# Scores as three half-word products from the sixth pair on, and another placing of the MoE units between the attention steps

## The chip, the cores and the metric

The kernel runs on one NeuronCore of a Trainium2 chip. The metric is the device time of one launch in microseconds (us). The engines are PE (TensorE: matrix products and transposes), DVE (VectorE), ACT (ScalarE), POOL (GpSimd) and SP (SyncE, which issues the DMAs). Each of them works through its own queue in the order in which the program put the instructions there, and they wait for each other by semaphores.

## The reference

```python
# q, k, v: (4, 8, 576, 64); x after attention: (4, 576, 512)
q_rot, k_rot = (rotate(q), rotate(k))
scores = scale * np.matmul(q_rot, k_rot.transpose(0, 1, 3, 2))
scores = scores - np.max(scores, axis=-1, keepdims=True)
attn = np.exp(scores)
attn = attn / (np.sum(attn, axis=-1, keepdims=True) + 1e-09)
attn_out = np.matmul(attn, v)
x = attn_out.transpose(0, 2, 1, 3).reshape(B, S, H * D)
h = np.maximum(x @ w_in, 0.0)              # w_in: 512 x 1024
conv_out = sum(conv_w[k] * shifted(h, k) for k in range(3))
gate = 1.0 / (1.0 + np.exp(-conv_out))
return h * gate @ w_out                    # w_out: 1024 x 512
```

## The kernel before

**Pairs and steps.** The 32 heads are taken as 16 pairs p. Each pair has five steps s: four blocks of 128 rows of q and, in step s = 4, the last 64 rows of both heads. A global step is n = 5p + s, 80 in all. In a step PE makes the scores of both heads (`emit_S`, L251, tiles `sp` from `qT` and `kT`), DVE takes the row maximum (L259, `negm`), and ACT the exponential (L263, `st`, or `str` for s = 4). PE turns the exponentials of the step before (`emit_T`, L311, tiles `tp`), and ACT copies them to `pt` (L189). What is left over of 64 key columns is turned apart (`emit_Trem`, L336), and DVE copies that to `pt` (L191). One head uses partitions 0 to 63 of `qT` and `kT`, the other 64 to 127, so a product of one head uses half of PE's rows.

**The product with v.** `emit_E` (L367) multiplies `pt` by v for the pair p in step 5(p+1), in two halves of 290 columns. A step with n divisible by five is called an E step below. ACT copies the results to `xn` (L377), DVE normalises them two or more steps later (L381), ACT and POOL split them in a high and a low part (L385, L386, tile `xT`).

**The wide stage and the switch.** Steps below `WIDE` = 26 use large PSUM tiles and run beside the conversion of the weights (`wsteps`, 64-bit to 32-bit, then high and low parts `winh`, `winl`, `wouth`, `woutl`, on ACT, DVE and POOL). At step 26 the PSUM is dealt out anew: two tiles `s` for scores, two `t` for transposes and E, two `m` for the MoE.

**The MoE.** From step 26 on, MoE units stand between the steps' other work. A block is 288 tokens. `emit_M1` (L400, an M1 unit) makes 128 of the 1024 hidden columns for a block in 12 products: (high weight, high x), (high weight, low x), (low weight, high x) for four slices of 128. The parts have the type float32r, where PE makes one pass. A plain float32 product is two passes and shows as two records. Each M1 unit is followed on other engines by a ReLU (ACT), three convolution steps (DVE), tanh (ACT), gate (DVE) and a split (ACT, POOL, tile `g`), each put off by so many ticks (`defer`). `emit_M2` (L478, an M2 unit) makes a quarter of an output tile, six products of 512 columns.

**Order.** `plan` holds (rank, function) for each step and `moe` the units of each step. The loop sorts by rank: scores 0, turning 1, exponentials 1.5, the rest 2; MoE units are set around the events of rank 2 and 4; E of the MoE stage has rank 10 and closes its step. The units of a block are spread over ten steps by a fraction x and a `room` of each step. Transposes of q and k (L224 to L233) are DVE's, at rank 0.45. The rotation (`rope`, L180, L183) is POOL's, at the end of a step. After step 86 comes the tail, blocks 6 and 7 of the MoE, with no attention beside it.

Of the kernel before, what the change touches and what calls it, by code (L numbers as in the profile page):

```python
# [20 lines left out]
def attention_moe_kernel(ctx, tc, q, k, v, w_in, conv_w, w_out, tab, tabx, out):  # L21
# [37 lines left out]
    rvc = [keep.tile([128, 32], F32, name=f"rvc_{s}") for s in range(2)]  # L59
    cw = keep.tile([128, 32], F32, name="cw")  # L60
    vrem = keep.tile([128, 2, D], F32, name="vr")
    strem = [keep.tile([128, S + 64], F32, name=f"str_{s}") for s in range(2)]
# [122 lines left out]
    QT, KT = {}, {}  # L185

# [8 lines left out]
    def qk_tiles(p):  # L195
        if p not in QT:
            QT[p] = p2.tile([128, S], F32, tag="qT", name="qT")
            KT[p] = p2.tile([128, S + 64], F32, tag="kT", name="kT")
# [21 lines left out]
    def emit_TQ(p, part):  # L220
        qk_tiles(p)
        x = raw.pop((p, part))[:, :, 0, :]
        if part == "q":
            nc.vector.transpose(out=QT[p].rearrange("p (c i) -> p c i", i=32), in_=x)  # L224
        else:
            kt = KT[p].rearrange("p (c i) -> p c i", i=32)
            nc.vector.transpose(out=kt[:, 2:20], in_=x)  # L227
            if p * STEPS < WIDE:
# [3 lines left out]
            if p * STEPS + STEPS > WIDE:  # L232
                nc.vector.transpose(out=kt[:, 0:2], in_=x[:, 16:18])  # L233
# [10 lines left out]
    def emit_S(p, s):  # L244
# [22 lines left out]
        if s < 4:  # L267
            st = ST[p, s] = p1.tile([128, 2, S], F32, tag="st", name="st", bufs=3)
        else:
            st = STR[p] = strem[p % 2][:, 0:S]  # L270
# [33 lines left out]
    def emit_T(p, s, h=None):  # L304
# [8 lines left out]
        if s == 4:  # L313
            st = strem[p % 2]
# [46 lines left out]
    def emit_E(p, j, a=0, n=XW):  # L361
        b, hp = divmod(p, NPB)
        xp = spare(n)
# [10 lines left out]
        if a == 0:  # L374
            xns[p, j] = p2.tile([128, XW], F32, tag="xn", name="xn", bufs=4)
# [218 lines left out]
    WIDE = 26  # L594
# [8 lines left out]
    def emit():  # L603
        with tc.manual_schedule(engines=engines):
            load0()
            for x in rvc + krem + [x[:, S:S + 64] for x in strem]:
# [23 lines left out]
            for p in range(NP):  # L630
# [10 lines left out]
                if n + 4 < WIDE:  # L641
                    for i in range(4):
                        at(n + 1 + i, 2, lambda p=p, i=i: emit_Trem(p, i, 1))
                else:
                    for i in range(2):
                        at(n + 2 + 2 * i, 2, lambda p=p, i=i: emit_Trem(p, 2 * i, 2))
# [8 lines left out]
                for j in range(2):  # L655
                    at(n + (9 if j and n + 8 < WIDE else 8), 1.7 + j, lambda p=p, j=j: norms.pop((p, j))())
# [7 lines left out]
            for blk in range(2 * B - 2):  # L664
                n0 = WIDE + MB * blk
                room = [0.5 if n % STEPS == 0 and n < STEPS * NP + 2 else 1.0 for n in range(n0, n0 + MB)]
                us = [(0.09 + 0.1 * f, lambda blk=blk, f=f: emit_M1(blk, f)) for f in range(NF)]
                if blk:
                    m2 = m2_units(blk - 1)
                    ne = 4 if blk % 4 == 0 else 0  # L670
                    us += [(0.05 * i if i < ne else 0.05 * ne + (1 - 0.05 * ne) * (i - ne) / (len(m2) - ne), u) for i, u in enumerate(m2)]
                for x, u in us:
                    y, k = x * sum(room), 0
# [115 lines left out]
```

## Time and profile before

| what | value |
|---|---|
| median of 3 runs | 516.81 us (515.56 to 519.25) |
| the profiled execution's own time | 514.66 us |
| its span, first to last instruction | 512.7 us |
| PE busy | 469.0 us, 91% of the span, 3880 products |
| DVE, ACT, POOL busy | 365.0, 311.8, 300.3 us |
| mean granted TensorE clock | 0.983 of full speed |

The span is what the rows of the trace add up to. The execution's own time is 1.96 us more, for what lies around it. The median of the timed runs is 2.15 us above the profiled execution. Busy time counts an instruction from start to end, and matrix products overlap, so lengths of work on PE are read as differences of start times.

### The profile page before, as it was taken

What the parts mean: (1) busy time and instruction counts of PE and PEld (TensorE: products, weight loads), DVE (VectorE), ACT (ScalarE), POOL (GpSimd) and SP (SyncE); (2) the same over time, 40 slices, a digit from 0 to 9 for tenths busy, and PEclk for the clock granted to TensorE, in tenths of its full rate; (3) what the DMA queues carried; (4) which work ended last, traced back from release to release, by engine and by line L of the source; (5) the groups of instructions that cost most, each with busy time, mean ns of one, the idle gap of its engine ahead of it and who ended that gap; (6) DMA issues with size and microseconds to landing.
All of it is one profiled execution on the core that took longest, in us unless ns stands there. A gap on an engine that the chain in (4) does not pass through costs nothing.

```text
span 512.7 us, 10801 instructions
## 1 busy us (share of the span) xinstructions
PE 469.0 (91%) x3880; PEld 350.0 (68%) x3880; DVE 365.0 (71%) x656; ACT 311.8 (61%) x821; POOL 300.3 (59%) x479
## 2 busy tenths in 40 slices
PE   1878789786999899999999999999999999999997
PEld 1445446553766587767878687868777676889986
DVE  5699889995597759684868487765868284748951
ACT  2588877885576767675667575754657564325520
POOL 3789988999576747646492829274573021314530
PEclk9999987997999999999999999999999999999999
DMA  8978965843424243433425251524220201000011
GB/s 225 178 128 165 191 158 140 188 113 76 88 47 94 47 93 68 93 69 73 90 49 90 63 100 45 88 73 88 51 68 1 68 1 46 22 21 22 1 42 60
DMA packets 139256, 42.61 MB, mean 83 GB/s; under 512 B 132012, under 2 KB 132804, under 8 KB 139204
## 3 DMA queue, kind: packets, MB, share of 16 engines
q1 hardware_dynamic: 137860, 41.54, 37.1%
q8 instruction: 30, 0.49, 0.4%
q10 hardware_dynamic: 1344, 0.39, 0.3%
q14 instruction: 22, 0.18, 0.1%
HBM read 37.12 MB, written 4.79 MB: 82 GB/s over the span
## 4 chain that ended last, share of the span: by engine, by line
PE 67%; DVE 13%; ACT 7%; POOL 5%; DMA 5%; issue 2%; SPq 0%; ACTq 0%; DVEq 0%; POOLq 0%
PE pm L400 13%; PE sp L251 12%; PE pm L478 11%; PE tp L367 11%; PE mt L478 8%; PE mt L400 5%; PE tp L311 5%; DVE negm L259 4%; ACT st L263 3%; ACT pt L189 2%; DMA rq<-q 2%; POOL rk L180 1%; DVE c L414 1%; POOL woutl L559 1%; DMA rk<-k 1%
## 5 line engine op out<-in xcount | busy, mean ns | idle before, releaser
L259 DVE TENSOR_REDUCE negm<-sp 128x1 f32<-128x576 f32 x144 | 102.4, 747 | 73.9 <-PE sp L251 66.6
L432 POOL TENSOR_TENSOR g<-c,g 128x288 fp32r<-128x288 f32 (+4 forms) x88 | 56.8, 658 | 154.6 <-ACT g L431 151.7
L189 ACT ACTIVATE pt<-tp 128x512 f32<-128x512 f32 (+3 forms) x176 | 84.4, 528 | 53.7 <-PE tp L311 53.3
L251 PE MATMUL sp<-kT,qT 64*128 64x288 f32 (+4 forms) x556 | 104.3, 474 | 6.4 <-DVE kT L227 3.2
L263 ACT ACTIVATE st<-sp,negm 128x576 f32<-128x576 f32 x128 | 94.0, 746 | 14.6 <-DVE negm L259 14.1
L400 PE MATMUL pm<-xT,winh 128*128 128x290 f32 x384 | 81.7, 305 | 0.0
L414 DVE SCALAR_TENSOR_TENSOR c<-rr,cw,c 128x288 f32<-128x288 f32 x128 | 77.6, 606 | 4.5
L251 PEld LDWEIGHTS sp<-kT,qT 64*128 64x128 f32 (+1 forms) x556 | 47.2, 179 | 33.5 <-issue 15.4
L478 PE MATMUL pm<-wouth,g 128*128 128x512 f32 x176 | 65.8, 415 | 0.0
L400 PEld LDWEIGHTS pm<-xT,winh 128*128 128x128 f32 x384 | 62.3, 189 | 3.2 <-issue 0.4
L311 PEld LDWEIGHTS tp<-idf,st 64*128 64x128 f32 x1024 | 42.5, 140 | 27.1 <-ACT st L263 16.2
L180 POOL TENSOR_TENSOR rq<-rq,tabt 128x192 f32<-128x192 f32 x90 | 56.8, 666 | 5.5 <-DMA rq<-q 5.3
L311 PE MATMUL tp<-idf,st 64*128 64x64 f32 x1024 | 49.4, 229 | 10.5 <-ACT st L263 10.4
L400 PE MATMUL pm<-xT,winl 128*128 128x290 f32 x192 | 56.7, 296 | 0.0
L367 PE MATMUL tp<-pt,vm 128*64 128x290 f32 x384 | 53.6, 422 | 3.4 <-ACT pt L189 3.4
L180 POOL TENSOR_TENSOR rk<-rk,tabt 128x192 f32<-128x192 f32 x90 | 56.6, 665 | 0.0
L423 DVE SCALAR_TENSOR_TENSOR c<-c,rr 128x288 f32<-128x288 f32 x64 | 36.6, 575 | 15.3 <-ACT c L420 15.3
L412 DVE TENSOR_SCALAR c<-rr,cw 128x288 f32<-128x288 f32 x64 | 33.3, 521 | 18.0 <-ACT rr L408 14.0
L386 POOL TENSOR_TENSOR xT<-xn,xT 128x290 fp32r<-128x290 f32 x32 | 29.6, 940 | 24.1 <-ACT xT L385 24.1
L367 PEld LDWEIGHTS tp<-pt,vm 128*64 128x64 f32 x384 | 27.0, 140 | 23.0 <-ACT pt L189 4.4
L420 ACT ACTIVATE c<-c 128x288 f32<-128x288 f32 x64 | 28.5, 445 | 17.7 <-DVE c L414 17.5
L478 PEld LDWEIGHTS pm<-wouth,g 128*128 128x128 f32 x176 | 33.0, 188 | 8.1
(102 smaller groups left out, 797.8 us busy)
## 6 DMA issues: line engine op xcount, KB each, us to landing
out<-ot SPq DMA_DIRECT2D x17, 256.0 KB
rq<-q SPq DMA_DIRECT2D x30, 144.0 KB
rq<-q SPq DMA_DIRECT2D x60, 72.0 KB
rk<-k SPq DMA_DIRECT2D x30, 144.0 KB
rk<-k SPq DMA_DIRECT2D x60, 72.0 KB
w<-moe_w_in SPq DMA_DIRECT2D x8, 512.0 KB
vm<-v SPq DMA_DIRECT2D x32, 128.0 KB
w<-moe_w_out SPq DMA_DIRECT2D x8, 512.0 KB
```

What stands on the lines that cost most here:

```text
L180: nc.gpsimd.tensor_tensor(out=y, in0=y, in1=tabt[:, a:a + 3], op=ALU.mult)
L189: nc.scalar.activation(out=out, in_=in_, func=AF.Copy, scale=1.0 if sc is None else sc)
L251: nc.tensor.matmul(out=out, lhsT=qt[64 * h:64 * h + 64, c], rhs=kt[64 * h:64 * h + 64, a:a + n], start=True, stop=True)
L259: reds.setdefault((p, s), []).append(lambda: nc.vector.tensor_reduce(out=nm, in_=sc, axis=AX.XY if len(sc.shape) == 3 else AX.X, op=ALU.ma ...
L263: lambda: nc.scalar.activation(out=dst, in_=sc, func=AF.Exp, bias=nm, scale=1.0, accum_out=sm)
L311: nc.tensor.transpose(ps[r][:, 64 * k:64 * k + 64], x[i], idf[i, i])
L367: nc.tensor.matmul(out=xp[64 * h:64 * h + 64, :], lhsT=vmain[p][:, h, i, :] if i < 4 else vrem[:, h, :], rhs=pt[:, 2 * i + h if i < 4 else ...
L400: nc.tensor.matmul(out=ps[:, 0:XW], lhsT=w[:, kk, fs], rhs=xT[:, xs, e, :], start=(i == 0), stop=(i == n - 1))
L414: nc.vector.scalar_tensor_tensor(out=c, in0=r[:, j + e:j + e + HS], scalar=cw[:, 8 * e + f:8 * e + f + 1], in1=c, op0=ALU.mult, op1=ALU.add,)
L423: nc.vector.scalar_tensor_tensor(out=c, in0=c, scalar=1.0, in1=r[:, j + 1:j + 1 + HS], op0=ALU.add, op1=ALU.mult)
L432: nc.gpsimd.tensor_tensor(out=lo, in0=c[:, o:o + n], in1=hi.bitcast(F32), op=ALU.subtract)
L478: nc.tensor.matmul(out=ops[tt][:, 0:width], lhsT=g_tile(tt, f, e), rhs=w[:, f, cols], start=(f == 0 and i == 0), stop=(f == NF - 1 and i = ...
```

## The change

From pair 5 on (all pairs whose last step lies at or beyond `WIDE`, which is now 25) the turned q and k go to one buffer each (`turnedq`, `turnedk`). ACT copies these, rounded, to a high part (`hq`, `hk`), and DVE subtracts that to get a low part (`lq`, `lk`). The scores are three float32r products, high by high, high by low and low by high, added up in PSUM. For s = 4 the two heads' 64 rows of q stand as a block diagonal in 128 rows, and the three products use all of PE's rows.

The MoE stage begins at step 25. The first block has 8 steps, the others ten; E steps have no room for units, so the 16 or 20 units of a block go to eight steps, evenly. Both halves of E stand in one E step, and the first uses an `m` tile in place of a `t` tile. `emit_Trem` turns one block in each of four steps, where the MoE stage had two in each of two. The normalisation of a pair moves from its step n+8 to n+7. Some buffers become fewer: `st` 3 to 2, `str` 2 to 1, `xn` 4 to 2.

```diff
+    def high_low(p, part, src):
+        hi, lo = (p2.tile(list(src.shape), F32R, tag=t + part, name=t + part) for t in "hl")
+        HI[p, part], LO[p, part] = hi, lo
+        defer(2, lambda: nc.scalar.activation(out=hi, in_=src, func=AF.Copy))
+        defer(4, lambda: nc.vector.tensor_tensor(out=lo, in0=src, in1=hi.bitcast(F32), op=ALU.subtract))
...
+        split = p * STEPS + STEPS > WIDE
...
+        def mms(items, c):
+            if (p, "q") not in HI:
+                for out, h, a, n in items:
+                    mm(out, h, a, n, c)
+                return
+            (qh, kh), (ql, kl) = ((t[p, "q"], t[p, "k"]) for t in (HI, LO))
+            for i, (x, y) in enumerate(((qh, kh), (qh, kl), (ql, kh))):
+                for out, h, a, n in items:
+                    r = slice(64 * h, 64 * h + 64)
+                    nc.tensor.matmul(out=out, lhsT=x[r, c], rhs=y[r, a:a + n], start=i == 0, stop=i == 2)
...
-                for h in range(2):
-                    mm(pss_[h][:, j, 0:HS], h, HS * j + 64 - 64 * h, HS, c)
+                mms([(pss_[h][:, j, 0:HS], h, HS * j + 64 - 64 * h, HS) for h in range(2)], c)
...
-            for h, j in ((0, 0), (1, 1), (0, 1), (1, 0)):
-                mm(ps[64 * h:64 * h + 64, j, 0:HS], h, HS * j + 64, HS, c)
+            for j in range(2):
+                for i, (x, y) in enumerate(((qh, kh), (qh, kl), (ql, kh))):
+                    nc.tensor.matmul(
+                        out=ps[:, j, 0:HS], lhsT=x[:, 512:640], rhs=y[:, HS * j + 64:HS * j + 64 + HS],
+                        start=i == 0, stop=i == 2,
+                    )
...
-        xp = spare(n)
+        xp = m_tile()[:, 0:n] if "m" in psum and j == 0 else spare(n)
...
-    WIDE = 26
+    WIDE = 25
...
-                n0 = WIDE + MB * blk
-                room = [0.5 if n % STEPS == 0 and n < STEPS * NP + 2 else 1.0 for n in range(n0, n0 + MB)]
+                n0 = WIDE + MB * blk - (MB - NF if blk else 0)
+                room = [float(n % STEPS != 0 or n > STEPS * NP) for n in range(n0, n0 + (MB if blk else NF))]
```

The scores of one ordinary step and what follows them on PE, before:

```order
L251 MATMUL sp<-kT,qT 128x288 x4
L311 MATMUL tp<-idf,st 128x64 x16
L478 MATMUL pm<-wouth,g 128x512
L478 MATMUL pm<-woutl,g 128x512
L478 MATMUL pm<-wouth,g 128x512 x2
L478 MATMUL pm<-woutl,g 128x512
L478 MATMUL pm<-wouth,g 128x512
```

And now, in a step of the same kind, the scores, the turning and the begin of the M1 unit that follows:

```order
L285 MATMUL sp<-hk,hq 128x288 x2
L285 MATMUL sp<-lk,hq 128x288 x2
L285 MATMUL sp<-hk,lq 128x288 x2
L285 MATMUL sp<-hk,hq 128x288 x2
L285 MATMUL sp<-lk,hq 128x288 x2
L285 MATMUL sp<-hk,lq 128x288 x2
L347 MATMUL tp<-idf,st 128x64 x16
L436 MATMUL pm<-xT,winh 128x290 x2
```

Four products of two passes have become twelve of one pass.

An E step without MoE units on PE, before (the end of the step ahead of it stands in the first two rows):

```order
L478 MATMUL pm<-wouth,g 128x512
L336 MATMUL tp<-idf,st 128x128 x2
L251 MATMUL sp<-kT,qT 128x288 x4
L311 MATMUL tp<-idf,str_82 128x64 x10
L367 MATMUL tp<-pt,vm 64x290 x8
L367 MATMUL tp<-pt,vr 64x290 x2
L367 MATMUL tp<-pt,vm 64x290 x8
L367 MATMUL tp<-pt,vr 64x290 x2
```

And every E step now:

```order
L372 MATMUL tp<-idf,st 128x128
L514 MATMUL pm<-wouth,g 128x512
L514 MATMUL pm<-woutl,g 128x512
L514 MATMUL pm<-wouth,g 128x512 x2
L514 MATMUL pm<-woutl,g 128x512
L514 MATMUL pm<-wouth,g 128x512
...
L347 MATMUL tp<-idf,str 128x64 x10
L403 MATMUL pm<-pt,vm 64x290 x8
L403 MATMUL pm<-pt,vr 64x290 x2
L403 MATMUL tp<-pt,vm 64x290 x8
L403 MATMUL tp<-pt,vr 64x290 x2
```

A unit now stands between the leftover transpose (L336, now L372) and the next step's scores, and the first half of E writes `pm` in place of `tp`.

DVE in a step in which k is turned, before:

```order
L259 TENSOR_REDUCE negm<-sp 128x1 x2
L227 STREAM_TRANSPOSE kT<-rk 128x576
L233 STREAM_TRANSPOSE kT<-rk 128x64
L412 TENSOR_SCALAR c<-rr_1703,cw 128x288
L414 SCALAR_TENSOR_TENSOR c<-rr_1703,cw,c 128x288 x2
L381 TENSOR_TENSOR xn<-xn,rb 128x290 x2
L259 TENSOR_REDUCE negm<-sp 128x1
```

And now:

```order
L291 TENSOR_REDUCE negm<-sp 128x1 x2
L246 STREAM_TRANSPOSE turnedk<-rk 128x576
L248 STREAM_TRANSPOSE turnedk<-rk 128x64
L199 COPY pt<-tp 128x128
L459 SCALAR_TENSOR_TENSOR c<-c,rr_1650 128x288
L193 TENSOR_TENSOR lk<-turnedk,hk 128x640
L448 TENSOR_SCALAR c<-rr_1647,cw 128x288
L450 SCALAR_TENSOR_TENSOR c<-rr_1647,cw,c 128x288 x2
L291 TENSOR_REDUCE negm<-sp 128x1
```

The subtraction for `lk` and a copy of a leftover transpose have come in between two maxima; the normalisation (`xn`) has gone to another step.

## Rows read from the trace of the kernel before

**Rows 1.** Stretch, length, busy PE, weight loads, DVE, ACT, POOL, then clock, DMA.

```profile
117.74:168.54 50.80, 46.43 (x385) 32.80 (x386) 35.31 (x65) 33.33 (x87) 35.18 (x65) 0.93 0.37 74
168.54:443.94 275.40, 268.32 (x2242) 204.78 (x2243) 188.88 (x350) 171.99 (x450) 142.76 (x223) 1.00 0.29 64
```

**Rows 2.** PE in order of time, steps 37 to 39: start, length, records.

```profile
184.69 1.24 PE L251 MATMUL sp<-kT,qT 64*128 64x288 f32 x8
185.77 0.66 PE L311 MATMUL tp<-idf,st 64*128 64x64 f32 x16
...
189.78 1.24 PE L251 MATMUL sp<-kT,qT 64*128 64x288 f32 x8
191.44 0.50 PE L478 MATMUL pm<-wouth,g 128*128 128x512 f32 x1
...
192.94 0.43 PE L400 MATMUL pm<-xT,winh 128*128 128x290 f32 x2
...
194.65 1.19 PE L251 MATMUL sp<-kT,qT 64*64 64x288 f32 x8
195.77 0.71 PE L311 MATMUL tp<-idf,st 64*128 64x64 f32 x16
```

**Rows 3.** PE in order of time, a short stretch inside the first scores of Rows 2.

```profile
185.04 0.65 PE L251 MATMUL sp<-kT,qT 64*128 64x288 f32 x4
```

**Rows 4.** PE in order of time, a float32 product of all rows in the wide stage.

```profile
118.80 0.49 PE L277 MATMUL sp<-kr,qT 128*128 128x128 f32 x2
119.12 0.27 PE L336 MATMUL sp<-idf,st 128*128 128x128 f32 x1
```

**Rows 5.** PE in order of time, E step 40, with an M1 unit.

```profile
199.83 1.24 PE L251 MATMUL sp<-kT,qT 64*128 64x288 f32 x8
...
201.30 0.54 PE L400 MATMUL pm<-xT,winh 128*128 128x290 f32 x2
...
203.11 2.17 PE L367 MATMUL tp<-pt,vm 128*64 128x290 f32 x16
...
208.14 1.24 PE L251 MATMUL sp<-kT,qT 64*128 64x288 f32 x8
```

**Rows 6.** All engines in order of time, E step 45, without a unit; idle before in brackets.

```profile
226.54 1.39 PE L251 MATMUL sp<-kT,qT 64*128 64x288 f32 x8
...
228.45 0.53 PE L311 MATMUL tp<-idf,str 64*128 64x64 f32 x9 [0.52 <-DVE pt L191]
...
229.45 2.17 PE L367 MATMUL tp<-pt,vm 128*64 128x290 f32 x16 [0.47 <-ACT pt L189]
...
234.48 1.24 PE L251 MATMUL sp<-kT,qT 64*128 64x288 f32 x8
```

**Rows 7.** PE in order of time, step 31, with one M1 unit.

```profile
155.34 1.24 PE L251 MATMUL sp<-kT,qT 64*128 64x288 f32 x8
...
159.62 1.72 PE L251 MATMUL sp<-kT,qT 64*128 64x288 f32 x7 [0.73 <-ACT st L263]
```

**Rows 8.** All engines in order of time, scores of steps 25, 26 and 27.

```profile
117.74 1.13 PE L251 MATMUL sp<-kT,qT 64*128 64x512 f32 x4 [1.62 <-DVE kT L227]
...
120.17 0.74 ACT L263 ACTIVATE str<-sp,negm 128x576 f32<-128x576 f32 x1
...
127.41 1.41 PE L251 MATMUL sp<-kT,qT 64*128 64x288 f32 x8
...
133.65 1.24 PE L251 MATMUL sp<-kT,qT 64*128 64x288 f32 x8
```

**Rows 9.** Busy time, columns as in Rows 1, around step 25.

```profile
121.00:128.00 7.00, 6.42 (x34) 3.32 (x36) 2.74 (x6) 4.02 (x14) 7.00 (x14) 0.51 0.27 47
```

**Rows 10.** Groups of instructions, each shape apart: busy, mean ns.

```profile
L381 DVE TENSOR_TENSOR xn<-xn,rb 128x290 f32<-128x290 f32 x32 | 15.1, 502 | 2.8 <-ACT xn L377 2.6
...
L556 ACT ACTIVATE winh<-wf 128x512 fp32r<-128x512 f32 x8 | 5.0, 630 | 2.3 <-DVE wf L513 2.2
```

**Rows 11.** DVE in order of time, maxima of step 43.

```profile
219.37 1.42 DVE L259 TENSOR_REDUCE negm<-sp 128x1 f32<-128x576 f32 x2 [1.24 <-PE sp L251]
```

More of the change, by code (lines that the diff above doesn't have):

```diff
@@ L59, in attention_moe_kernel @@
     rvc = [keep.tile([128, 32], F32, name=f"rvc_{s}") for s in range(2)]
+    turned = {part: keep.tile([128, S + 64], F32, name=f"turned{part}") for part in "qk"}
     cw = keep.tile([128, 32], F32, name="cw")
     vrem = keep.tile([128, 2, D], F32, name="vr")
-    strem = [keep.tile([128, S + 64], F32, name=f"str_{s}") for s in range(2)]
+    strem = [keep.tile([128, S + 64], F32, name="str")]
     xT = keep.tile([128, NSLOT, 2, XW], F32R, name="xT")
@@ L196, in qk_tiles @@
         if p not in QT:
-            QT[p] = p2.tile([128, S], F32, tag="qT", name="qT")
-            KT[p] = p2.tile([128, S + 64], F32, tag="kT", name="kT")
+            QT[p] = wkeep.tile([128, S], F32, tag="qT", name="qT", bufs=2)
+            KT[p] = wkeep.tile([128, S + 64], F32, tag="kT", name="kT", bufs=2)
     def emit_TQ0(part):
@@ L220, in emit_TQ @@
     def emit_TQ(p, part):
-        qk_tiles(p)
         x = raw.pop((p, part))[:, :, 0, :]
-        if part == "q":
-            nc.vector.transpose(out=QT[p].rearrange("p (c i) -> p c i", i=32), in_=x)
-        else:
-            kt = KT[p].rearrange("p (c i) -> p c i", i=32)
-            nc.vector.transpose(out=kt[:, 2:20], in_=x)
-            if p * STEPS < WIDE:
+        split = p * STEPS + STEPS > WIDE
+        if split:
+            dst = turned[part]
+        else:
+            qk_tiles(p)
+            dst = (QT if part == "q" else KT)[p]
+        to = dst.rearrange("p (c i) -> p c i", i=32)
+        if part == "q":
+            if split:
+                nc.vector.transpose(out=to[:, 0:16], in_=x[:, 0:16])
+                for h in range(2):
+                    r = slice(64 * h, 64 * h + 64)
+                    nc.vector.transpose(out=to[r, 16 + 2 * h:18 + 2 * h], in_=x[r, 16:18])
+            else:
+                nc.vector.transpose(out=to, in_=x)
+        else:
+            nc.vector.transpose(out=to[:, 2:20], in_=x)
+            if split:
+                nc.vector.transpose(out=to[:, 0:2], in_=x[:, 16:18])
+            else:
                 for h in range(2):
@@ L231, in emit_TQ @@
                     nc.vector.transpose(out=krem[p % 2][r, r].rearrange("p (c i) -> p c i", i=32), in_=x[r, 16:18])
-            if p * STEPS + STEPS > WIDE:
-                nc.vector.transpose(out=kt[:, 0:2], in_=x[:, 16:18])
+        if split:
+            high_low(p, part, dst)
     ST, STR = {}, {}
@@ L247, in emit_S @@
             sums[p] = p2.tile([128, 9], F32, tag="sums", name="sums")
-        qt, kt = QT[p], KT[p]
+        qt, kt = QT.get(p), KT.get(p)
         def mm(out, h, a, n, c):
@@ L267, in emit_S @@
         if s < 4:
-            st = ST[p, s] = p1.tile([128, 2, S], F32, tag="st", name="st", bufs=3)
+            st = ST[p, s] = p1.tile([128, 2, S], F32, tag="st", name="st", bufs=2)
         else:
-            st = STR[p] = strem[p % 2][:, 0:S]
+            st = STR[p] = strem[0][:, 0:S]
         if "m" not in psum:
@@ L374, in emit_E @@
         if a == 0:
-            xns[p, j] = p2.tile([128, XW], F32, tag="xn", name="xn", bufs=4)
+            xns[p, j] = p2.tile([128, XW], F32, tag="xn", name="xn", bufs=2)
         xn = xns[p, j]
@@ L605, in emit @@
             load0()
-            for x in rvc + krem + [x[:, S:S + 64] for x in strem]:
+            for x in [turned["q"]] + rvc + krem + [x[:, S:S + 64] for x in strem]:
                 nc.vector.memset(x, 0.0)
@@ L640, in emit @@
                         at(m + 1, 0 if m + 1 < WIDE else 1, lambda p=p, s=s, h=h: emit_T(p, s, h))
[L641 to L646, printed above, removed]
+                for i in range(4):
+                    at(n + 1 + i, 2, lambda p=p, i=i: emit_Trem(p, i, 1))
                 if n + 8 < WIDE:
@@ L655, in emit @@
                 for j in range(2):
[L656 removed]
+                    at(n + (9 if j else 8) if n + 8 < WIDE else n + 8 - (n + 5 >= WIDE), 1.7 + j, lambda p=p, j=j: norms.pop((p, j))())
             nw = len(wsteps)
@@ L670, in emit @@
                     ne = 4 if blk % 4 == 0 else 0
-                    us += [(0.05 * i if i < ne else 0.05 * ne + (1 - 0.05 * ne) * (i - ne) / (len(m2) - ne), u) for i, u in enumerate(m2)]
-                for x, u in us:
-                    y, k = x * sum(room), 0
+                    us += [(0.05 * i if i < ne else 0.05 * ne + (1 - 0.05 * ne) * (i - ne + 0.5) / (len(m2) - ne), u) for i, u in enumerate(m2)]
+                us.sort(key=lambda e: e[0])
+                for i, (x, u) in enumerate(us):
+                    y, k = (i + 0.5) / len(us) * sum(room), 0
                     while y >= room[k]:
```

9 lines of the change are left out of this document (6 added, 3 removed).

## The prediction

> **What bounds the kernel now.** I read the stretches first, then PE in order of time. In the stretch from step 34 to the tail, 275.40 us long, PE is busy for 268.32 us, DVE for 188.88 and ACT for 171.99 [rows 1]. So PE is the bound there, and what counts is what each piece costs on PE from start to start. An ordinary step with one M1 and one M2 unit, step 38, goes from 189.78 to 194.65, 4.87 us, and nothing is idle in it. Step 37, with two leftover transposes besides, takes 189.78 - 184.69 = 5.09, so such a transpose costs 0.11. Scores take 185.77 - 184.69 = 1.08 (s = 4: 195.77 - 194.65 = 1.12), an M2 unit 192.94 - 191.44 = 1.50, an M1 unit 194.65 - 192.94 = 1.71, of which about 1.60 are its 12 products, 0.134 each, and 0.11 the wait before the next scores [rows 2].
>
> PE isn't the bound in two places. One is an E step without a unit. Step 40, with an M1 unit, takes 208.14 - 199.83 = 8.31; less its M1 unit, 203.11 - 201.30 = 1.81, that is 6.50 [rows 5]. Step 45 has no unit and takes 234.48 - 226.54 = 7.94: the transposes wait 0.52 for DVE, which empties the leftover transpose, E waits 0.47 for ACT, which empties the transposes, and the scores are slow too [rows 6]. There are five such steps (35, 45, 55, 65, 75), 1.1 to 1.6 over 6.50, 7.0 us in all. The other is a step with one unit, as 31: 159.62 - 155.34 = 4.28 for some 3.4 us of work, and its successor waits for the exponentials [rows 7]. Six steps before 34 are of this kind, each about 1 us over its work. The switch itself is a third place: from the scores of step 25 to those of 27 it is 133.65 - 117.74 = 15.9 us [rows 8], at a granted clock of 0.51 for 7 us of it, the 1.2 GHz level, after PE had been waiting for `kT` [rows 8, 9].
>
> **Scores.** A float32 step has 8 records. Four of them begin by 185.04 in two pairs, and from 185.04 on three pairs take 185.77 - 185.04 = 0.73, 0.243 a pair; the first pair takes 0.35, 0.11 more, for the load of its weights after a product of another shape [rows 2, 3]. The two heads of a pair run side by side: a float32 record of all rows costs (119.12 - 118.80)/2 = 0.16 for 128 columns [rows 4], where one of these costs 0.12 for 288. The new step has 12 records, six pairs of one pass. No row shows a float32r product on half of the rows. From below, a pair costs half of a two-pass pair, 0.122; from above, 0.134 for each head apart, 0.27 a pair, if they don't run together. I take 0.134 a pair, what one float32r product of 290 columns costs, since float32 pairs do run together. A step then costs 6 x 0.134 + 0.11 = 0.91 in place of 1.08: 0.17 less, in 43 steps from 26 on, 7.3 us (with 0.122: 10). For s = 4 six full-row products cost 0.80 in place of 1.12: 0.32 in 11 steps, 3.5 us. Sum: -10.8.
>
> The Trainium skill speaks against this, in the page "TensorE: Matmul & The Clock Gate", section "Part 3: Packing small matmuls — row/col tiling": a weight load overlaps a running matmul only where the row group differs. The new pairs come one after the other on the same two row groups, so each pair's loads would lie open by it. The trace of before doesn't agree for float32, whose pairs on the same groups follow at 0.243 with no room for a load [rows 3]; the result by that rule is the second rival.
>
> **E steps.** All 11 E steps beside scores are now without a unit. What made the five wait is treated twice: a unit of 1.5 us now stands between the leftover transpose and the next scores, so DVE's copy has 2.4 us in place of 1.1; and the first half of E takes an `m` tile, so it needn't wait until ACT has emptied the transposes, whose copies only the second half needs, 2.5 us later. I take 6 of the 7.0 us as gone. If only the first cure works, E still waits about half a us in 11 steps and the gain is 2. Norms one step earlier have E's 5 us and the next steps before them; I cost them at nothing.
>
> **Steps with one unit.** The first block now has 8 units in six steps, two of them with two: four light steps (26, 28, 29, 32) in place of six. -2 us, -1 to -3.
>
> **The switch.** Step 25's scores now need the new PSUM, so they come after the exponentials of step 24 (which begin at 120.17 and take 0.74 [rows 8]) and after two more copies on ACT and DVE for k's parts: about 122 in place of 117.74. Then both halves of E follow in that step, 6.6 us at full clock, partly at half of it as E was before [rows 9]. I get the scores of step 26 at 131.6 and of 27, with one M1 unit done, at 136, where before they stood at 133.65 with the same work done. +2.4, from -1 (a warm clock) to +5. The zeroing of `rr` on POOL moves ahead of 5 us of rotation, which takes away a wait of the first convolution, off this path.
>
> **Added work elsewhere.** For each pair ACT makes two copies of 640 columns. One of 512 takes 0.63 [rows 10], so 0.63 to 0.79 each, 1.5 a pair. DVE makes two subtractions of 640, from 0.50 (that of 290 [rows 10]) to 1.11 (in proportion), say 0.85, and splits a transpose and two copies in smaller ones: 2.4 us a pair, 1.3 to 3.4. Four units a pair in each of them, where before it was five and three, make the load even. DVE's 188.88 in 275.40 is 69% [rows 1]; nine and a half pairs at 2.4 add 23, and the stretch gets shorter, so some 83%. ACT goes from 62% to 73%. What covers this is that DVE sits at the maxima and waits for scores, as 1.24 us in step 43 [rows 11]. But the subtraction for k stands there between two maxima, and waits for its copy on ACT; behind it are the convolution, the next maximum, then the exponentials, for which the scores after that wait. The leftover transpose also takes a `t` tile in four steps of five, not two, and the next step's transposes wait for DVE's copy of it. I put +4 on this, about 0.1 a step; from 0 to +10, which is 0.2 in each of 49 steps.
>
> **Rest.** Smaller buffers (`st`, `str`, `xn`) are read a step before they are written again; the tail is unchanged, but its first M2 units come nearer to the last M1 unit, within a us. Both at nothing.
>
> **Sum.** -10.8 - 6 - 2 + 2.4 + 4 = -12.4 on the profiled 514.66: 502.3. The median of the runs lies 2.15 above that execution, so I forecast 504.4, say 504.
>
> **Rivals.** First, DVE becomes what PE waits for. For it: 83% on an engine whose instructions wait in order; against it: an M1 unit in each of steps 37 to 39 and no idle PE there [rows 2]. The added stalls are then 10 to 12 instead of 4: 511. Second, the pairs' weight loads lie open, slower than before: each pair costs 0.134 + 0.11 = 0.24, six of them 1.45, 0.37 more than the 1.08 of now. 43 steps cost 16 more where I take off 7.3; s = 4 keeps its gain, as full-row M1 products at 0.134 hide their loads. 504 + 23 = 527. It decides against the change from about 0.22 a pair on, where the other gains are used up. Were the heads not to run together, it would be 539. For it: no row shows such products; against it: the float32 pairs [rows 3]. Third, E steps wait as before, all 11 at 1.4: 15.4 in place of the 1 left above, 518. For it: six of them lose the unit that covered them [rows 5]; against it: the new tile. Last, all goes well, 0.122 a pair and no stalls: 493.
>
> **Chances.** Forecast 0.60, DVE 0.19, open loads 0.06, E steps 0.07, all well 0.08. About 1% is what a measurement of this kernel can tell from no change, 511.6 on the fast side. Nearly all of the forecast, all of the best case and most of DVE's lie below it: faster 0.77; the rest of DVE's and most of the E case within 1%: 0.15; slower 0.08. The range leaves out the open loads, the E case and half of the best: 496 to 513.
>
> **What would show it.** In the trace after: 12 score records a step with 0.9 us from the first to the turning; E steps of 6.3 to 6.6; ordinary steps of 4.7 to 4.85; the scores of step 27 near 136. Wrong if score pairs stand 0.2 or more apart, if PE's idle time names DVE's copies or subtractions in most steps, or if the switch loses more than 5 us.

## The result, and the profile after

The changed kernel takes 522.24 us (521.07 to 523.47, six runs) and the kernel before, on the same chip, 515.55 (515.22 to 519.25): a ratio of 1.0115, with a 95% interval of 1.0084 to 1.0146. It is slower by 1.15%, where 504 us was predicted. The profiled span is 520.7 us, against 512.7.

I cut each trace at the starts of the scores of steps 25, 36 and 79. The columns are the times between these cuts, in us; the experiments that stand below are in the table too.

| kernel | to step 25 | 25 to 36 | 36 to 79 | from 79 on | span | median |
|---|---|---|---|---|---|---|
| before | 117.7 | 62.1 | 238.9 | 94.0 | 512.7 | 515.6 |
| after | 126.0 | 69.9 | 238.4 | 86.4 | 520.7 | 522.2 |
| no wait (`early_no_wait`) | 124.4 | 67.9 | 229.0 | 86.4 | 507.7 | 508.9 |
| late (`lo_late`) | 122.3 | 63.0 | 226.7 | 86.4 | 498.4 | 501.3 |
| no subtraction (`no_sub`) | 122.3 | 62.6 | 226.8 | 86.3 | 497.9 | 499.6 |

What was won is in the last column: the MoE's blocks begin earlier, so that fewer units are left for the steps behind 79 (the tail itself, blocks 6 and 7, is 68.8 and 68.9 us). What was lost stands in the first two, and the long third one, in which the scores and the E steps were to give most, gave 0.5 us. Not all of the first column is the kernels' own: step 22 begins at 105.81 in the change and at 103.28 in the late version, so 2.5 of the 3.7 us between these two arise where they have the same instructions. From 82 to 90 us the granted clock is 0.71 in the change and 1.00 in the late version.

The stretches of the change, columns as in [rows 1], show it from the side of PE:

```profile
126.02:195.92 69.90, 62.78 (x538) 49.48 (x538) 51.85 (x96) 43.31 (x109) 44.53 (x76) 0.87 0.28 55
195.92:434.30 238.38, 230.11 (x2120) 185.65 (x2119) 187.08 (x357) 163.57 (x419) 130.06 (x197) 1.00 0.32 69
```

In the second PE is idle for 8.3 us (238.38 - 230.11; before it was 3.5 in the same steps, 238.89 - 235.42), and DVE is busy for 78% of it (187.08/238.38). In the first the granted clock is 0.87 of full speed.

The scores themselves are as forecast. PE in order of time, step 36 of the change (L285 are the scores, L347 the turning), answers to [rows 2, 3]:

```profile
195.92 0.40 PE L285 MATMUL sp<-hk,hq 64*128 64x288 f32 x2
196.16 0.30 PE L285 MATMUL sp<-lk,hq 64*128 64x288 f32 x2
196.29 0.29 PE L285 MATMUL sp<-hk,lq 64*128 64x288 f32 x2
196.43 0.29 PE L285 MATMUL sp<-hk,hq 64*128 64x288 f32 x2
...
196.82 0.66 PE L347 MATMUL tp<-idf,st 64*128 64x64 f32 x16
...
200.72 0.40 PE L285 MATMUL sp<-hk,hq 64*128 64x288 f32 x2
```

The second pair begins 0.24 after the first and the others 0.13 to 0.14 apart; the scores take 0.90 and the whole step 4.80. But only two steps of these five, 36 and 37, are so short. All engines in order of time, steps 37 to 40 of the change (L192 is the copy of the high part, L193 the subtraction, L448 and L450 the convolution, L291 the maximum, L295 the exponential, L332 the scores for s = 4; in brackets the idle time before and its releaser):

```profile
200.53 0.76 ACT L192 ACTIVATE hq<-turnedq 128x640 fp32r<-128x640 f32 x1
...
201.32 0.83 DVE L193 TENSOR_TENSOR lq<-turnedq,hq 128x640 fp32r<-128x640 f32 x1 [1.57 <-ACT hq L192]
...
202.47 1.07 DVE L450 SCALAR_TENSOR_TENSOR c<-rr,cw,c 128x288 f32<-128x288 f32 x2
...
203.46 1.41 DVE L291 TENSOR_REDUCE negm<-sp 128x1 f32<-128x576 f32 x2
...
206.69 0.76 PE L347 MATMUL tp<-idf,st 64*128 64x64 f32 x16
...
207.58 1.93 DVE L450 SCALAR_TENSOR_TENSOR c<-rr,cw,c 128x288 f32<-128x288 f32 x2
...
209.44 1.41 DVE L291 TENSOR_REDUCE negm<-sp 128x1 f32<-128x576 f32 x2
...
211.16 0.40 PE L332 MATMUL sp<-hk,hq 128*128 128x288 f32 x1 [0.40 <-ACT st L295]
...
211.92 0.29 PE L332 MATMUL sp<-hk,lq 128*128 128x288 f32 x1
...
212.79 0.82 DVE L193 TENSOR_TENSOR lk<-turnedk,hk 128x640 fp32r<-128x640 f32 x1 [0.59 <-ACT hk L192]
213.53 0.92 DVE L448 TENSOR_SCALAR c<-rr,cw 128x288 f32<-128x288 f32 x1
214.48 1.50 DVE L450 SCALAR_TENSOR_TENSOR c<-rr,cw,c 128x288 f32<-128x288 f32 x2
215.91 0.74 DVE L291 TENSOR_REDUCE negm<-sp 128x1 f32<-128x576 f32 x1
...
216.69 0.74 ACT L295 ACTIVATE str<-sp,negm 128x576 f32<-128x576 f32 x1 [0.17 <-DVE negm L291]
...
217.57 0.40 PE L285 MATMUL sp<-hk,hq 64*128 64x288 f32 x1 [1.08 <-ACT str L295]
```

Read it from the bottom. PE waits 1.08 us in the E step because the exponentials of step 39 are late. They are late because their maximum starts at 215.91, although the last of those scores began at 211.92. In between DVE stood still for 0.59 for ACT's copy of k, subtracted, and did three pieces of the convolution, all of which stand in its queue ahead of the maximum. One step earlier the maxima of step 38 start at 209.44, though the last of that step's scores were under way when the turning (L347) began at 206.69; that is 3.94 after the first score of 205.50. The change's order makes only a part of this: in the kernel with late subtractions below it is 3.24 (198.15 - 194.91), for there too the convolution ahead of these maxima takes 1.93. In step 37 DVE stood still for 1.57 us in the change, because `lq` waits for a copy that on ACT stands behind two exponentials and a ReLU. When it was free, most of that step's scores were done, and the subtraction and the convolution still came first: the maxima begin 2.74 after the scores (203.46 - 200.72). Before, DVE at its maxima waited for the scores, as in [rows 11]; now the scores, by way of the exponentials, wait for DVE. The waits of the stretch from 196 to 430 in the change's trace, as us in all, how often, longest:

```profile
PE sp L285 <- ACT str L295: 5.0, 6, 1.1
PE sp L332 <- ACT st L295: 1.7, 4, 0.6
DVE lq L193 <- ACT hq L192: 11.4, 8, 1.7
DVE lk L193 <- ACT hk L192: 3.4, 7, 0.6
```

The E steps, which [rows 5, 6] show at 7.94 and 8.31, are from step 40 to 75 at 7.2 to 7.8 in six of eight and at 6.34 in two. The switch, to be set against [rows 8]: scores of step 25 at 126.02 (forecast 122), of 26 at 134.64 (131.6), of 27 at 138.09 (136).

### The profile page after: what moved, and what is told of

Same layout as the page of the kernel before. It is cut to its first block, busy times and chain, and to the rows that moved or that the text cites. A ratio compares the mean times of both kernels' runs of the same rounds, so it can differ in the third digit from the quotient of the medians.

```text
span 520.7 us, 11167 instructions
## 1 busy us (share of the span) xinstructions
PE 468.5 (90%) x4036; PEld 363.9 (70%) x4036; DVE 392.5 (75%) x720; ACT 325.2 (62%) x843; POOL 304.9 (59%) x479
## 3 DMA queue, kind: packets, MB, share of 16 engines
HBM read 37.12 MB, written 4.79 MB: 80 GB/s over the span
## 4 chain that ended last, share of the span: by engine, by line
PE 49%; DVE 28%; ACT 14%; issue 5%; DMA 2%; POOL 1%; SPq 0%; DVEq 0%; ACTq 0%; POOLq 0%
DVE negm L291 8%; PE pm L403 7%; PE mt L514 6%; PE pm L436 6%; PE sp L285 6%; ACT st L295 6%; PE tp L403 6%; PE mt L436 5%; DVE c L450 5%; PE pm L514 5%; PE tp L347 4%; DVE c L448 3%; PE sp L272 2%; ACT pt L197 2%; DVE wt L544 2%
## 5 line engine op out<-in xcount | busy, mean ns | idle before, releaser
L291 DVE TENSOR_REDUCE negm<-sp 128x1 f32<-128x576 f32 x144 | 102.3, 746 | 35.8 <-PE sp L285 26.5
L468 POOL TENSOR_TENSOR g<-c,g 128x288 fp32r<-128x288 f32 (+4 forms) x88 | 58.7, 678 | 101.0 <-ACT g L467 95.8
L295 ACT ACTIVATE st<-sp,negm 128x576 f32<-128x576 f32 x128 | 93.8, 742 | 27.5 <-DVE negm L291 27.4
L450 DVE SCALAR_TENSOR_TENSOR c<-rr,cw,c 128x288 f32<-128x288 f32 x128 | 83.3, 651 | 4.5
L436 PE MATMUL pm<-xT,winh 128*128 128x290 f32 x384 | 85.7, 316 | 0.3 <-ACT rr L444 0.3
L422 POOL TENSOR_TENSOR xT<-xn,xT 128x290 fp32r<-128x290 f32 x32 | 28.4, 889 | 77.8 <-ACT xT L421 71.1
L181 POOL TENSOR_TENSOR rq<-rq,tabt 128x192 f32<-128x192 f32 x90 | 59.6, 695 | 5.5 <-DMA rq<-q 5.5
L347 PE MATMUL tp<-idf,st 64*128 64x64 f32 x1024 | 49.0, 231 | 13.1 <-ACT st L295 12.2
L347 PEld LDWEIGHTS tp<-idf,st 64*128 64x128 f32 x1024 | 42.6, 143 | 21.6 <-ACT st L295 17.0
L285 PE MATMUL sp<-hk,hq 64*128 64x288 f32 x176 | 39.4, 352 | 10.8 <-ACT str L295 6.7
L448 DVE TENSOR_SCALAR c<-rr,cw 128x288 f32<-128x288 f32 x64 | 33.6, 525 | 16.1 <-ACT rr L444 16.1
L285 PEld LDWEIGHTS sp<-hk,hq 64*128 64x128 f32 x176 | 22.0, 189 | 29.7 <-issue 8.5
L436 PEld LDWEIGHTS pm<-xT,winl 128*128 128x128 f32 x192 | 37.5, 196 | 0.0
L272 PE MATMUL sp<-kT,qT 64*128 64x512 f32 (+2 forms) x120 | 34.3, 667 | 2.2 <-DVE kT L246 1.5
```

Of the source, the lines that this page charges most:

```text
L181: nc.gpsimd.tensor_tensor(out=y, in0=y, in1=tabt[:, a:a + 3], op=ALU.mult)
L285: nc.tensor.matmul(out=out, lhsT=x[r, c], rhs=y[r, a:a + n], start=i == 0, stop=i == 2)
L291: reds.setdefault((p, s), []).append(lambda: nc.vector.tensor_reduce(out=nm, in_=sc, axis=AX.XY if len(sc.shape) == 3 else AX.X, op=ALU.ma ...
L295: lambda: nc.scalar.activation(out=dst, in_=sc, func=AF.Exp, bias=nm, scale=1.0, accum_out=sm)
L347: nc.tensor.transpose(ps[r][:, 64 * k:64 * k + 64], x[i], idf[i, i])
L436: nc.tensor.matmul(out=ps[:, 0:XW], lhsT=w[:, kk, fs], rhs=xT[:, xs, e, :], start=(i == 0), stop=(i == n - 1))
```

## The experiments

My theory after the two traces was the order: on DVE the subtraction waits for ACT's copy and holds up the next maxima, which stand behind it. The rivals were the load (DVE's added work in all, wherever it stands) and the placing (no units in E steps, two or three elsewhere). If nothing else is said, all but the edit is as in the change. The kernel before took 516.65 to 517.36 us beside these runs, and the ratios are against that.

**Where the subtraction stands (`lo_late`).** It goes behind the maxima of the next step.

```diff
-        defer(4, lambda: nc.vector.tensor_tensor(out=lo, in0=src, in1=hi.bitcast(F32), op=ALU.subtract))
+        at(late["n"] + 1, 0.25, lambda: nc.vector.tensor_tensor(out=lo, in0=src, in1=hi.bitcast(F32), op=ALU.subtract))
```

> The subtractions stay on DVE, but each is put behind the maxima of the next step instead of ahead of them. Theory 1 (order): as if they were off DVE, 500 to 508 us, steps as for the kernel with POOL. Theory 2 (load): DVE's work is the same, 516 to 522. Theory 3 (placing): within 3 us of 522.

Measured: 501.29 us, a ratio of 0.9695 (0.9644 to 0.9747), the lowest time here of a kernel that does the whole work. One moved line gives back 21 us. DVE in order of time, step 37 of this kernel and the maxima of step 38:

```profile
190.10 0.37 DVE L448 TENSOR_SCALAR c<-rr,cw 128x288 f32<-128x288 f32 x1 [0.95 <-ACT rr L444]
190.51 1.07 DVE L450 SCALAR_TENSOR_TENSOR c<-rr,cw,c 128x288 f32<-128x288 f32 x2
191.50 1.42 DVE L291 TENSOR_REDUCE negm<-sp 128x1 f32<-128x576 f32 x2
192.83 0.81 DVE L193 TENSOR_TENSOR lq<-turnedq,hq 128x640 fp32r<-128x640 f32 x1
...
198.15 1.41 DVE L291 TENSOR_REDUCE negm<-sp 128x1 f32<-128x576 f32 x2
```

The scores of the step begin at 190.11 and the maxima 1.39 later; in the change it was 203.46 - 200.72 = 2.74. The subtraction waits for nothing. All E steps from 40 on are at 6.3, and the stretches show PE idle for only 1.6 us in 226.70, although DVE has the same work and is busy for a larger share, 185.52/226.70 = 82%:

```profile
122.31:185.32 63.01, 58.29 (x539) 46.10 (x540) 51.06 (x96) 43.17 (x109) 42.90 (x72) 0.94 0.31 61
185.32:412.02 226.70, 225.07 (x2119) 183.76 (x2118) 185.52 (x358) 162.17 (x419) 132.54 (x203) 1.00 0.33 73
```

In the first of the two the granted clock is 0.94, in the change it was 0.87. An estimate from these rows: (1 - 0.87) x 69.90 = 9.1 us of full clock are missing there in the change and (1 - 0.94) x 63.01 = 3.8 here, so of the 6.9 us between the two in the steps 25 to 36 up to 5.3 went by way of the clock.

**The subtraction on POOL (`lo_pool`).**

```diff
-        defer(4, lambda: nc.vector.tensor_tensor(out=lo, in0=src, in1=hi.bitcast(F32), op=ALU.subtract))
+        defer(4, lambda: nc.gpsimd.tensor_tensor(out=lo, in0=src, in1=hi.bitcast(F32), op=ALU.subtract))
```

> The two subtractions for the low parts go from DVE to POOL; all else as in the changed kernel. Theory 1 (the subtraction waits for ACT's copy and holds up the next maxima behind it on DVE): steps in which k is turned fall from 5.65 to about 4.8, E steps from 7.8 to about 6.4, the steps after the switch gain too: 498 to 506 us. Theory 2 (DVE has too much work, in whatever order): it loses 1.7 us of work a pair, 505 to 512. Theory 3 (the placing of the units and the single-unit steps after the switch): within 3 us of 522.

Measured: 517.98, ratio 1.0017 (0.9997 to 1.0037), outside all three ranges. DVE has neither the work nor the wait, and still only 4 us come back, where the order theory had forecast 498 to 506. In order of time, first PE at the switch, then DVE and POOL in step 37:

```profile
128.76 0.61 PE L285 MATMUL sp<-lk,hq 64*128 64x288 f32 x2 [4.10 <-POOL lk L193]
...
201.21 2.25 DVE L450 SCALAR_TENSOR_TENSOR c<-rr,cw,c 128x288 f32<-128x288 f32 x2
201.47 1.67 POOL L193 TENSOR_TENSOR lq<-turnedq,hq 128x640 fp32r<-128x640 f32 x1 [1.56 <-ACT hq L192]
...
203.37 1.41 DVE L291 TENSOR_REDUCE negm<-sp 128x1 f32<-128x576 f32 x2
```

At the switch PE waits 4.10 us for `lk`, and step 25 is 13.4 long, where it is 8.6 in the change. Later the two convolution pieces, 1.07 above, take 2.25 beside POOL's subtraction, so that the maxima begin 2.56 after the scores of 200.81, nearly as late as in the change. So this run doesn't decide on DVE's queue as the cause: the subtraction left it, but what stayed got slower and `lk` came late. The runs that follow decide.

**One of the two late (`q_late`, `k_late`).** The moved line of `lo_late` for q alone; in the second kernel it says "k".

```diff
-        defer(4, lambda: nc.vector.tensor_tensor(out=lo, in0=src, in1=hi.bitcast(F32), op=ALU.subtract))
+        sub = lambda: nc.vector.tensor_tensor(out=lo, in0=src, in1=hi.bitcast(F32), op=ALU.subtract)
+        if part == "q":
+            at(late["n"] + 1, 0.25, sub)
+        else:
+            defer(4, sub)
```

> Only q's subtraction goes behind the next maxima, k's stays where the change has it. If the wait for ACT's copy is the cost, it goes by the waits seen (q 11.4 us in 8 pieces, k 3.4 in 7): 77% of the 21 us come back, 506. If the place is the cost, q and k count alike: 511 to 512.

> Only k's subtraction goes behind the next maxima, q's stays. By the waits for ACT's copy: 23% of the 21 us come back, 517. By the place alone: 511 to 512. If k's matters more because the E step follows behind it: 508 or less.

Measured: 513.22, ratio 0.9916 (0.9884 to 0.9949), and 508.93, 0.9845 (0.9789 to 0.9901). Moving q's gives 9.0 us and k's 13.3, which add up to 22.3, about the 21 of both. The forecast by the waits seen was the wrong way round: k's wait is the shorter one (3.4 us against 11.4), but behind it stands the E step, as the bottom of the list of steps 37 to 40 shows. The traces agree: with only q's moved, PE still waits 6.3 us (7 times) for `str` in the E steps and 0.3 for `st` ahead of s = 4; with only k's moved it is 0.3 and 1.8 (4 times). DVE waits for the copy that stayed as long as in the change, 3.4 and 11.4 us. So a wait of DVE costs by what stands behind it and not by its length alone.

**The same work early, without the wait (`early_no_wait`).** The subtraction takes the turned q or k from itself, so the low parts are zero here; the products with them are still made, and step 36 is 4.79 long as in the late version.

```diff
-        defer(4, lambda: nc.vector.tensor_tensor(out=lo, in0=src, in1=hi.bitcast(F32), op=ALU.subtract))
+        defer(4, lambda: nc.vector.tensor_tensor(out=lo, in0=src, in1=src, op=ALU.subtract))
```

> The changed kernel (522.2) with both subtractions at their old place and of their old length, but taking the turned q or k from itself, so that they wait for no copy; the low parts are left out of the result by that (they are zero). DVE has the same work in the same order as in the change. If the waits for ACT's copy are what takes DVE's time (14.8 us in the trace of the change from 196 to 440, and more before): 503 to 509. If the subtractions' own length in that place counts as much: 510 to 516. If neither does: 520.

Measured: 508.93, ratio 0.9839 (0.9805 to 0.9873). DVE's order and work are those of the change; only the wait for ACT's copy is gone, and 13.3 of the 21 us with it. DVE in order of time, step 37:

```profile
196.19 0.83 DVE L193 TENSOR_TENSOR lq<-turnedq 128x640 fp32r<-128x640 f32 x1
197.10 0.37 DVE L448 TENSOR_SCALAR c<-rr,cw 128x288 f32<-128x288 f32 x1
197.51 1.07 DVE L450 SCALAR_TENSOR_TENSOR c<-rr,cw,c 128x288 f32<-128x288 f32 x2
198.50 1.41 DVE L291 TENSOR_REDUCE negm<-sp 128x1 f32<-128x576 f32 x2
```

The subtraction fills the time in which DVE would have waited anyway for the ReLU (ACT L444) that L448 needs, and the maxima come 1.38 after the scores of 197.12, as in the late version. What is left over against the late version is 7.6 us by the medians and 9.3 by the spans. Of the 9.3, 4.9 lie in the steps 25 to 36 (67.9 against 63.0), 2.3 after 36, in four E steps of 6.9, and 2.1 ahead of step 23, where the two kernels do the same.

**No subtraction (`no_sub`).** The products take the high part in place of the low one.

```diff
-        hi, lo = (p2.tile(list(src.shape), F32R, tag=t + part, name=t + part) for t in "hl")
-        HI[p, part], LO[p, part] = hi, lo
+        hi = p2.tile(list(src.shape), F32R, tag="h" + part, name="h" + part)
+        HI[p, part], LO[p, part] = hi, hi
...
-        defer(4, lambda: nc.vector.tensor_tensor(out=lo, in0=src, in1=hi.bitcast(F32), op=ALU.subtract))
```

> The changed kernel with no subtraction at all: the products take the high part in place of the low one, so PE's work is the same and DVE has 22 instructions of 0.82 us less; the low parts are left out of the result. If late subtractions lie wholly in DVE's free time: 500 to 502, as late. If each us of DVE counts in the steps of a pair's turning, even late: 490 to 497, about as much less as the doubled late subtractions (515.1) are more.

Measured: 499.63, ratio 0.9663 (0.9628 to 0.9699). The 22 late subtractions cost 1.7 us in all, which is within what the intervals leave open. The 22.6 us of the early ones (522.24 - 499.63) are thus: 13.3 for the wait, 7.6 for the place, 1.7 for the rest. The change and these kernels ran on different chips, on which the kernel before took 515.55 to 517.36; by the ratios (1.0115, 0.9839, 0.9695, 0.9663, each of 517 us) the parts are 14.3, 7.4 and 1.7. Each ratio's interval is 1.6 to 2.7 us to either side, so the sizes are known to a few us. `early_dummy` below, by another edit, puts the same early work without the wait at 9.0.

**Twice the work, early and late (`early_dummy`, `late_twice`).** A second subtraction of the same size is added to the late version, once at the old place, once in front of the late one. The line for the first:

```diff
+        defer(4, lambda: nc.vector.tensor_tensor(out=lo, in0=src, in1=src, op=ALU.subtract))
```

> The late subtractions (501.3) with a second subtraction of the same size added on DVE at the old place, in front of the next step's maxima; it reads only the turned q or k, not ACT's copy, and its result is overwritten by the true one later. So the place and the length of the early work are those of the change, and the wait for the copy is gone. If it is the wait for ACT's copy that cost the 21 us: 500 to 505. If it is the place of 0.8 us of work ahead of the maxima, whatever it waits for: 514 to 522, or more, as DVE now has 15 more such instructions. In the changed kernel's trace the waits for copies sum to 14.8 us over 15 pieces from 196 to 440 and the subtractions themselves to 12.3, so if each counts by its length: about 511.

> The late subtractions (501.3), each preceded at the same late place by a second one of the same size whose result is overwritten. DVE has as much added work as in the version with an early dummy (510.3), but none of it ahead of a maximum of the same step. If that version's 9 us are the place: 501 to 504 here. If they are the sum of DVE's work: 508 to 512.

Measured: 510.29, ratio 0.9845 (0.9790 to 0.9901), and 515.06, 0.9960 (0.9930 to 0.9990). The first fits a cost by length, the second neither theory: if the place alone counted, it should have been free. Its waits from 185 to 430 (its lines stand one further down, L194 is the subtraction) name what happened:

```profile
PE sp L333 <- ACT st L296: 3.3, 6, 0.8
PE sp L286 <- DVE lk L194: 3.2, 5, 0.9
```

Pushed back by the one ahead of it, the true `lk` is now late for its own pair's first scores, and the exponentials before s = 4 are late again. Behind the maxima there is room for one subtraction, not for two; so "late costs nothing" holds for this length only. More work on DVE thus costs time late as well, through what stands behind it; that the sum of DVE's work counts as such isn't shown. How the 13.8 us divide between the two waits and the steps before 36 (66.8 us there, against 63.0) I can't say.

**The placing (`placing_alone`, `split_old_placing`, `late_old_placing`).** The first has float32 scores with no parts, but the change's switch at 25, placing, E tiles and buffers. The other two have the change's split scores, early or late, with the placing formulas of before:

```diff
...
-                room = [float(n % STEPS != 0 or n > STEPS * NP) for n in range(n0, n0 + (MB if blk else NF))]
-                us = [((f + 0.5) / NF, lambda blk=blk, f=f: emit_M1(blk, f)) for f in range(NF)]
...
+                room = [0.5 if n % STEPS == 0 and n < STEPS * NP + 2 else 1.0 for n in range(n0, n0 + MB)]
+                us = [(0.09 + 0.1 * f, lambda blk=blk, f=f: emit_M1(blk, f)) for f in range(NF)]
...
```

> Float32 scores as before, no parts, no subtraction; switch at 25, placing of the units, E tiles and small buffers as in the changed kernel. Theories 1 and 2: ordinary steps near 4.98, E steps 6.5, little loss after the switch: 505 to 512 us. Theory 3: E steps of 7.5 and more and slow steps after the switch stay, 518 to 526.

> Scores in three products and the switch at 25, but the units placed by the formulas of before (ten steps a block, half a room in E steps). Theory 1: the subtractions still hold up the maxima, 514 to 524 us. Theory 2: the load comes in bursts of five and three units again, 520 to 528. Theory 3: 504 to 511.

> The late subtractions with the placing formulas of the kernel before (units in E steps at half weight, ten steps from 25 on). With float32 scores the new placing was worth 11.9 us (505.3 against 517.2), with early subtractions 13.3 (535.5 against 522.2). If the placing is worth the same beside late subtractions: 512 to 515. By the prediction's terms (E steps 6, one-unit steps 2): 507 to 510. If the old placing was only bad because of the early subtractions: 501 to 504.

Measured: 505.34, ratio 0.9774 (0.9731 to 0.9817); 535.49, 1.0342 (1.0284 to 1.0399); 519.28, 1.0066 (1.0024 to 1.0107). The placing is worth 11.9 us with float32 scores (there together with the switch, the E tiles and the buffers), 13.3 beside early subtractions and 18.0 beside late ones. It isn't the part that made the change slow. The last two times lie above all that was expected for them: the old placing is worse beside the split scores than I thought, and why isn't shown. With the old placing even the late version is no faster than the kernel before. In `placing_alone` an ordinary step is 4.97, in the late version 4.80: the split scores' 0.17 a step is there as forecast.

**The tile of E's first half (`late_e_t`).** The late version with a `t` tile for it, as before.

```diff
-        xp = m_tile()[:, 0:n] if "m" in psum and j == 0 else spare(n)
+        xp = spare(n)
```

> The late subtractions, with the first half of E in a t tile again, as in the kernel before; all else as in the late version. The prediction put 4 of its 6 us for the E steps on the m tile: 505. If the unit between the leftover transpose and the scores does it all: 501 to 502. If E waits as it did before in every one of the 11 steps: 511 or more.

Measured: 511.05, ratio 0.9875 (0.9812 to 0.9938), 9.8 us more than the late version. PE in order of time, E step 40, of the late version (the first half of E writes `pm`, with no wait) and of this kernel (it writes `tp`):

```profile
204.80 0.40 PE L285 MATMUL sp<-hk,hq 64*128 64x288 f32 x2
...
206.10 2.18 PE L403 MATMUL pm<-pt,vm 128*64 128x290 f32 x16
...
211.13 0.40 PE L285 MATMUL sp<-hk,hq 64*128 64x288 f32 x2
```
```profile
208.14 0.40 PE L285 MATMUL sp<-hk,hq 64*128 64x288 f32 x2
...
210.04 2.17 PE L403 MATMUL tp<-pt,vm 128*64 128x290 f32 x16 [0.53 <-ACT pt L197]
...
215.07 0.40 PE L285 MATMUL sp<-hk,hq 64*128 64x288 f32 x2
```

The step is 6.33 against 6.93: the wait for ACT of [rows 6] is back in every E step, 0.6 each. There are 12 E steps from 25 to 80, 7.2 of the 9.8 us; 1.9 arise before step 24, where the two kernels have the same instructions: the granted clock is 0.83 from 82 to 90 us, and 1.00 in the late version. So much of a difference between two of these kernels can come from such a stretch alone.

**Ten steps for the first block (`lo_late_ten`).** The late version, whose first block has ten steps like the others.

```diff
-                n0 = WIDE + MB * blk - (MB - NF if blk else 0)
-                room = [float(n % STEPS != 0 or n > STEPS * NP) for n in range(n0, n0 + (MB if blk else NF))]
+                n0 = WIDE + MB * blk
+                room = [float(n % STEPS != 0 or n > STEPS * NP) for n in range(n0, n0 + MB)]
```

> The late subtractions, and the first block's eight M1 units spread over ten steps (from 25 on) like all later ones, not over six. The steps 26 to 35 of the late version take 3.5 to 7.1 us, and two units in a step stand there with 1.9 us convolutions ahead of the maxima. If those crowded steps cost time: 3 to 6 us less than the late version, 495 to 498. If PE's sum of work counts: the same, 500 to 503, since steps with one unit are added.

Measured: 502.26, ratio 0.9704 (0.9661 to 0.9748), not told apart from the late version. That doesn't show that a crowded first block is free, for the edit moves all later blocks by two steps as well: cut as in the table, this kernel takes 60.2 us from step 25 to 36 (late version 63.0), 224.5 from 36 to 79 (226.7) and 91.7 behind 79 (86.4). What the looser blocks give comes back as units left for the end.

## Why the prediction was wrong

**The step that failed** is the one under "Added work elsewhere": "I put +4 on this, about 0.1 a step; from 0 to +10". The place and the chain were named there for k (its subtraction stands between two maxima, waits for its copy on ACT, and behind it are the convolution, the next maximum, the exponentials and the scores); q's subtraction, which alone is worth 9.0 us (`q_late`), wasn't named. Its size was not worked out from any row but from the share that DVE is busy and the 1.24 us of [rows 11], which are free only if DVE waits with nothing queued ahead of the maximum. The share of 83% comes out a little high, too: with the forecast's 12.4 us off the stretch it is (188.88 + 23)/(275.40 - 12.4) = 81%. The subtractions alone measured 22.6 us, as `no_sub` shows: 13.3 for the wait, 7.6 for the place, 1.7 for the rest. The term of 4 replaced by 22.6 turns the forecast of 504 into 522.6, and 522.24 was measured; that it comes so near is luck, for two other errors cancel in it (see the sum below).

**Bound and ordinary step.** Right for the steps without a late maximum: PE bounds them, and 4.78 to 4.80 (steps 36 and 37 of the change) lies in the forecast 4.7 to 4.85. Step 38 of the change takes 5.66.

**Scores.** Right for the pairs (0.134 forecast, 0.13 to 0.14 seen) and their step. For s = 4 the gain was over-sized: from the first score to the turning it is 200.85 - 199.87 = 0.98 in the late version, not 0.80. The -10.8 came out as -5.7 by the medians (505.34 for `placing_alone`, 499.63 for `no_sub`) and -7.8 by the spans; ACT's copies for the parts are counted in this.

**E steps.** The cure works only where the exponentials are in time: 6.33 in the late version (forecast 6.3 to 6.6), 7.2 to 7.8 in most of the change's. The tile does more of it than the 4 us I gave it, 0.6 in every E step.

**The switch and the steps with one unit.** In the late version the scores of steps 25, 26 and 27 begin at 122.3, 130.5 and 133.9, by the forecast 122, 131.6 and 136. In the change all three are 2 to 4 us later than the forecast. A part of that is lost ahead of the switch. Against the late version it is 2.5 us before step 22, as said above, and 1.6 in step 23, in which the change's first subtraction stands: it is 5.96 long there and 4.40 in the late version. The -2 for one-unit steps is not shown: `lo_late_ten` differs by 1.0 us from the late version, within the intervals, and moves the later blocks too.

**The sum.** Without the failing term the forecast is 500.4, and `no_sub` gave 499.63. That it fits so well is luck: the scores gave less than I took off (5.7, not 10.8), and the placing more (11.9 for it, its tiles and the switch, where -6, -2 and +2.4 make -5.6).

**Rivals.** The first rival was the nearest: DVE is what PE waits for, with 10 to 12 us named for it. But its reason, a share of 83%, is not the cause: the late version has DVE at 82% and is the fastest, the change has 78% and is the slower of the two. What counts is what stands ahead of the maxima in two steps of five. Nor did the sign named for it show: PE's waits name ACT's exponentials, not DVE's copies or subtractions. The open loads didn't come about: the pairs follow each other on the same row groups at 0.13 to 0.14 us, although a load takes 0.18 there. The rule of the Trainium skill that stands in the prediction (page "TensorE: Matmul & The Clock Gate", section "Part 3: Packing small matmuls — row/col tiling") doesn't hold for them. The spacing from which open loads would have decided against the change comes out of the prediction's terms at 0.20 a pair, not 0.22: the other terms win 12.4 - 7.3 = 5.1 us, 0.12 for each of 43 steps, so six pairs may take 1.20. Nor did the E case: the E steps wait for the exponentials, not for `tp`.

## What to carry to other kernels

An engine with free time in the mean can still be the bound in the steps where its queue holds a piece that waits for another engine ahead of the piece that the critical engine waits for. As an upper bound, price such a piece by its own length plus the wait in front of it, times the number of steps, less what a row shows the engine to stand still there anyway. Here that is 22 subtractions of 0.82, 18.0 us, and at least the 14.8 us of waits listed above (11.4 + 3.4), 32.8 in all, where 22.6 were measured. And put such a piece behind the critical one if its own user comes later. Moving one line (`lo_late`) made of a change that lost 1.15% one that gains 3%.

## What the runs showed of the hardware

How long DVE's convolution takes goes with what POOL does beside it. Two pieces took 1.07 us at 202.47 in the change, where POOL did nothing (it was idle for the 6.76 us before 206.56), and 1.93 at 207.58. POOL in order of time around the latter:

```profile
206.56 0.81 POOL L422 TENSOR_TENSOR xT<-xn,xT 128x290 fp32r<-128x290 f32 x1 [6.76 <-ACT xT L421]
207.32 0.88 POOL L468 TENSOR_TENSOR g<-c,g 128x288 fp32r<-128x288 f32 x1
208.17 1.03 POOL L422 TENSOR_TENSOR xT<-xn,xT 128x290 fp32r<-128x290 f32 x1
```

With POOL's subtraction beside it (`lo_pool`) it was 2.25. The Trainium skill's page "GPSIMD Engine Reference", section "8. Key points", says that POOL shares its SBUF interfaces with DVE and that DVE instructions with two SBUF inputs contend with it; these rows agree.

A wait of PE in E step 35 cost twice. In the change PE waits 1.64 us for the exponentials, and the granted clock falls to the 1.2 GHz level, 0.50 in the stretch from 189.00 to 192.40:

```profile
187.97 0.40 PE L285 MATMUL sp<-hk,hq 64*128 64x288 f32 x1 [1.64 <-ACT str L295]
...
189.42 3.65 PE L403 MATMUL pm<-pt,vm 128*64 128x290 f32 x16
```

The 16 products take 3.65 us where they take 2.18 at full clock, and the step is 9.99 long, against 7.09 in the late version. There PE waits 0.33 us at the same place, and the granted clock is 1.00 for the whole step.
